# One head per q piece, six rows at a time, and each head's k_m standing twice

## The chip, the cores and the metric

The kernel runs on one core of a Trainium2 chip. Its engines work from queues of their own, each in order: TensorE for matmuls (PE, and PEld for its weight loads), VectorE (DVE), ScalarE (ACT), GpSimd (POOL) and SyncE (SP), which here only issues DMAs. The metric is the device time of one execution in microseconds (us); lower is better. The inputs are the same for both kernels.

## The reference

Three stages follow each other. For each of 8 batches and 8 heads, attention over 576 rows goes through 32 memory slots; its output is the input of a two-layer network (512 to 2048 to 512, squared ReLU), and that one's output goes through a layer of 8 experts in which each of the 4608 tokens takes the best one.

```python
a = exp(phi - max(phi, axis=2)); a = a / (sum(a, axis=2) + 1e-9)     # over the 576 rows
k_m = einsum('bhsm,bhsd->bhmd', a, k)                                 # 32 x 64 per head
v_m = einsum('bhsm,bhsd->bhmd', a, v)
scores = (q @ k_m.T) / 8                                              # 576 x 32 per head
attn = softmax(scores, axis=-1)
x = (attn @ v_m)                                                      # -> [4608, 512]
x = relu(x @ w_in) ** 2 @ w_out
e = argmax(x @ w_gate); g = softmax gate
out = g * (relu(x @ w1[e]) @ w2[e])
```

## The kernel before

A batch's attention is a generator, `attention(b)`, whose steps are spread over the steps of the network's main loop. phi, k and v of a batch come with six neighbouring rows of a head to a partition (96 partitions times 6 rows make the 576). `s_kv(g)` makes k_m and v_m of four heads (a group g); `s_tr(g)` turns them and multiplies by a mask, so that `kb` holds the k_m of two heads at a time as diagonal blocks, and `vbd` the v_m.

q comes in pairs of heads, 4 pairs to a batch and 32 in all (`load_q`, lines 324 to 329). The tile is [96, 6, 2, 64]: for row j of a partition the 64 numbers of one head stand beside the 64 of the other. So the DMA (one for each head, line 328, 144 KB) reads 1536 neighbouring bytes of a partition and writes them as six pieces of 256 bytes. `s_q(pr)` turns a row j of both heads at a time into [128, 96] (line 436) and copies three of these from PSUM (line 441). `s_soft(g)` makes the scores of one half of the rows j for both pairs of a group (line 457: 12 matmuls to a PSUM bank), then the maximum, the subtraction and the exponential of that half (lines 465 to 469), and, after both halves, the sum, the reciprocal and the product (472 to 475). `s_back(g)` turns the result, one half of the rows after the other (line 483), into `attnT`. `u_steps` multiplies v_m into w_in and leaves U (lines 541 to 557), so that a main-loop step n needs U and attnT of the batch whose tokens it reads.

The main loop has 192 steps: 12 blocks of 384 tokens by 16 slices of 128 hidden columns. `g1(n)` is the first layer (line 637, PE; ReLU and squares on ACT at 645 to 648, the low half of g on DVE at 649), and `g2`, three steps behind, adds into three PSUM banks (line 657, 9 matmuls to a step). Ahead of it w_in and w_out come through a ring of four buffers (`raw_ring`, line 215) and are converted from 64-bit numbers (ACT line 234, DVE lines 235 to 237). Beside the main loop runs `weight_stream`: it loads the experts' weights (`wstage`, lines 569 and 571, 512 KB each), finds their maximum or norm (DVE line 180, ACT 588), splits them into two halves of 16 bits (ACT 615, DVE 616) and stores them again (`ws`, line 617). Each block is then routed (`route`): its rows are turned by DMA transposes (line 729), which give the logits (787).

From about 848 us the experts' tiles run (lines 961, 973, 988, 1001, 92), with their DMAs in an order written out by hand.

The order on every other engine is not the order of the code. A scheduler orders all instructions by a model of their durations, DMAs included, and by what they need; then each engine's queue is fixed, SP's too. A DMA that waits for something holds all later ones on SP, and an instruction that waits holds all later ones of its engine. Tiles of one tag in a pool share buffers, and the next user waits for the last reader. Each DMA from SP takes the next of eight completion semaphores in turn.

## Time and profile before

| | |
|---|---|
| median of 3 runs | 1315.33 us (1314.53 to 1315.97) |
| the profiled execution's own time | 1313.53 us |
| its span, first to last instruction | 1311.5 us |
| TensorE clock granted, mean share | 0.953 |
| busy over the span | PE 89%, PEld 47%, DVE 50%, ACT 50%, POOL 9% |
| moved by DMA | 205.25 MB in 264,370 packets, mean 156 GB/s |
| HBM | 234.53 MB read, 55.76 MB written |

Busy shares are means over stages with different limits: loading and converting w_in and w_out (to 103 us), the main loop with attention and the weight stream (to about 600), the main loop almost alone (to 848), the experts. So the views by stretch of time and the chain of waits say more than the shares. A PE span ends where a model says, so a PE that is shown as busy need not be at its peak. A DMA share of 1.0 means that all 16 DMA engines were busy; it can pass 1 somewhat.

### The profile page before, as it was taken

What the parts mean: (1) busy time and instruction counts of PE and PEld (TensorE: products, weight loads), DVE (VectorE), ACT (ScalarE), POOL (GpSimd) and SP (SyncE); (2) the same over time, 40 slices, a digit from 0 to 9 for tenths busy, and PEclk for the clock granted to TensorE, in tenths of its full rate; (3) what the DMA queues carried; (4) which work ended last, traced back from release to release, by engine and by line L of the source; (5) the groups of instructions that cost most, each with busy time, mean ns of one, the idle gap of its engine ahead of it and who ended that gap; (6) DMA issues with size and microseconds to landing.
All of it is one profiled execution on the core that took longest, in us unless ns stands there. A gap on an engine that the chain in (4) does not pass through costs nothing.

```text
span 1311.5 us, 21652 instructions
## 1 busy us (share of the span) xinstructions
PE 1172.5 (89%) x7306; PEld 615.5 (47%) x7306; DVE 659.2 (50%) x1676; ACT 649.6 (50%) x1315; POOL 120.9 (9%) x169
## 2 busy tenths in 40 slices
PE   1537998999998998999999999989999998889896
PEld 0414555545455555466565565434433443334342
DVE  5788977779778767775646344350111111101100
ACT  2458886798777877776656566411111111111111
POOL 2000101101011101011010000031000100000000
PEclk9558998999999998999999999999998999999998
DMA  6956749468879579673131011585467466794762
GB/s 183 261 196 195 198 149 260 153 202 247 222 236 239 195 237 245 188 202 66 25 80 25 25 50 24 164 180 126 105 149 150 97 156 151 159 245 105 157 153 61
DMA packets 264370, 205.25 MB, mean 156 GB/s; under 512 B 209855, under 2 KB 228287, under 8 KB 264256
## 3 DMA queue, kind: packets, MB, share of 16 engines
q1 hardware_dynamic: 257616, 182.67, 55.2%
q0 software_dynamic: 6640, 21.16, 4.6%
q8 instruction: 59, 0.97, 0.3%
q14 instruction: 55, 0.45, 0.1%
HBM read 234.53 MB, written 55.76 MB: 221 GB/s over the span
## 4 chain that ended last, share of the span: by engine, by line
PE 33%; issue 33%; DMA 15%; DVE 9%; ACT 5%; POOL 3%; SPq 0%; POOLq 0%; ACTq 0%; DVEq 0%
PE acc L657 17%; PE h L637 9%; DMA wstage<-in_moe_w_dram 5%; DMA ws<-wo 3%; POOL out_dram L92 3%; DMA raw_ring<-in_moe_w_in_dram 2%; DVE wo L616 2%; DMA e_t<-in_phi_dram 2%; ACT wo L615 1%; DMA xTb<-rec 1%; PE e L961 1%; PE st L457 1%; PE u L541 1%; PE u L550 1%; PE kvm L367 1%
## 5 line engine op out<-in xcount | busy, mean ns | idle before, releaser
L657 PE MATMUL acc<-wo,g 128*128 128x512 f16 x1728 | 419.9, 382 | 1.9 <-ACT x2f L695 1.4
L657 PEld LDWEIGHTS <-g 128*128 128x128 f16 x1728 | 167.4, 99 | 175.1 <-issue 12.4
L988 PE MATMUL e<-w2t,gT 128*128 128x512 f16 x936 | 217.3, 389 | 25.1 <-DMA gT<-g 21.6
L637 PE MATMUL h<-attnT,U 128*128 128x384 f16 (+1 forms) x1536 | 234.6, 290 | 5.6 <-ACT U L556 5.4
L961 PE MATMUL e<-w1t,xT 128*128 128x512 f16 x936 | 210.5, 380 | 8.1 <-DMA w1t<-ws 5.6
L973 DVE SCALAR_TENSOR_TENSOR g<-e,g 128x512 f16<-128x512 f32 x78 | 50.3, 686 | 298.3 <-ACT g L972 298.2
L637 PEld LDWEIGHTS <-U 128*128 128x128 f16 x1536 | 141.5, 100 | 91.5 <-issue 19.4
L988 PEld LDWEIGHTS <-gT 128*128 128x128 f16 x936 | 92.8, 100 | 144.2 <-DMA gT<-g 25.7
L649 DVE TENSOR_TENSOR g<-r,g 128x384 f16<-128x384 f32 x192 | 106.1, 555 | 95.4 <-ACT r L648 94.5
L961 PEld LDWEIGHTS <-xT 128*128 128x128 f16 x936 | 91.4, 98 | 120.7 <-issue 10.0
L645 ACT ACTIVATE r<-h 128x384 f32<-128x384 f32 x192 | 92.6, 485 | 80.4 <-PE h L637 72.6
L1001 ACT ACTIVATE y<-e,fac 128x512 f32<-128x512 f32 x39 | 26.8, 688 | 207.7 <-PE e L988 199.2
L972 ACT ACTIVATE g<-e 128x512 f16<-128x512 f32 x78 | 42.3, 595 | 168.4 <-PE e L961 168.4
L647 ACT ACTIVATE g<-r 128x384 f16<-128x384 f32 x192 | 99.9, 522 | 12.3 <-PE acc L657 8.5
L648 ACT ACTIVATE r<-r 128x384 f32<-128x384 f32 x192 | 99.8, 520 | 3.6
L616 DVE SCALAR_TENSOR_TENSOR wo<-wstage,wsc,wo 128x1024 f16<-128x1024 f32 x64 | 81.0, 1276 | 22.8 <-ACT wo L615 22.8
L615 ACT ACTIVATE wo<-wstage,wsc 128x1024 f16<-128x1024 f32 x64 | 71.9, 1144 | 38.0 <-DMA ws<-wo 21.8
L92 POOL DMA_INDIRECT out_dram<-y,rt x39 | 37.9, 971 | 380.1 <-ACT y L1001 374.2
L92 POOL DMA_INDIRECT scr<-rec,sl x36 | 36.8, 1023 | 281.4 <-ACT r L645 97.9
L367 PE MATMUL kvm<-kv,e_t 128*32 128x128 f32 x768 | 28.2, 293 | 31.8 <-ACT e_t L352 27.4
L180 DVE TENSOR_REDUCE wm<-wstage 128x1 f32<-128x1024 f32 x32 | 38.8, 1212 | 15.4 <-DMA wstage<-in_moe_w_dram 15.4
L457 PE MATMUL st<-kb,qT 128*96 128x64 f32 x384 | 42.0, 266 | 3.5 <-DVE attnT L488 3.5
(241 smaller groups left out, 1077.3 us busy)
## 6 DMA issues: line engine op xcount, KB each, us to landing
w1t<-ws SPq DMA_DIRECT2D x144, 512.0 KB
w2t<-ws SPq DMA_DIRECT2D x144, 512.0 KB
wstage<-in_moe_w_dram SPq DMA_DIRECT2D x64, 512.0 KB
ws<-wo SPq DMA_DIRECT2D x64, 512.0 KB
kv<-in_k_dram SPq DMA_DIRECT2D x16, 576.0 KB
kv<-in_v_dram SPq DMA_DIRECT2D x16, 576.0 KB
q<-in_q_dram SPq DMA_DIRECT2D x64, 144.0 KB
raw_ring<-in_moe_w_in_dram SPq DMA_DIRECT2D x16, 512.0 KB
```

Of the source, the lines that this page charges most:

```text
L92: i = G.indirect_dma_start(out=dst[:, :], out_offset=bass.IndirectOffsetOnAxis(ap=index, axis=0), in_=src, in_offset=None, bounds_check=bo ...
L457: T.matmul(bank[:PS, j * P + 64 * x:j * P + 64 * x + 64], qTs[2 * g + x][:, jj * PS:(jj + 1) * PS], kbd[g][:, 64 * x:64 * x + 64], start=T ...
L615: A.activation(hi, src, AF.Copy, scale=s)
L616: V.scalar_tensor_tensor(lo, src, s, hi, ALU.mult, ALU.subtract)
L637: T.matmul(bank[:, off:off + w], u_t[b][:, g, uh, f * P:(f + 1) * P], attnT[b][:, g, ah, s0:s0 + w], start=(x == 0), stop=(x == len(seq) - 1),
L645: A.activation(r, bank[:, 0:BLK], AF.Relu, scale=2.0 ** -10)
L647: A.activation(g[:, 0], r, AF.Square)
L648: A.activation(r, r, AF.Square)
L649: V.tensor_tensor(g[:, 1], r, g[:, 0], op=ALU.subtract)
L657: T.matmul(a, g[:, gh, tt * P:(tt + 1) * P], wo[:, f, wh, :], start=(f == 0 and x == 0), stop=(f == NF - 1 and x == 2),)
L961: T.matmul(bank[hf], x[:, 4 * xh + c, :].bitcast(F16), w[c][:, wh * F + hf * 512:wh * F + (hf + 1) * 512], start=(c == 0 and xh == 0 and w ...
L988: T.matmul(a, gT[:, 8 * gh + f, :], w[f // 2][:, o:o + DM], start=(f == 0 and x == 0), stop=(f == 7 and x == 2),)
```

## The change

- q of a pair of heads is one tile [96, 2, 6, 64] and one DMA: the six rows of a head stay together, 1536 bytes to a piece.
- `s_q` turns two neighbouring rows of one head at a time, so the upper 64 partitions of a turned piece hold one row and the lower 64 the next.
- `kb` therefore holds each head's k_m twice, over the upper and the lower rows: [128, 4, 2, 32] in place of [128, 128], one multiplication by a broadcast mask.
- `s_soft` goes by pair x of heads in place of halves of the rows: 6 matmuls for a bank from one pair's `qT`, and operations on 4-dimensional strided pieces of `pt`. The numbers of matmuls, ACT and DVE instructions are the same.
- `mx` and `es` share one buffer.

```diff
@@ -323,9 +323,11 @@
 
     def load_q(n):
         b, pr = divmod(n, 4)
-        t = ps.tile([PS, NJ, 2, D], F32, tag="q", name=f"q{n}", bufs=2)
-        for h in range(2):
-            SP.dma_start(t[:, :, h, :], q[b, 2 * pr + h].rearrange("(p j) d -> p j d", p=PS))
+        t = ps.tile([PS, 2, NJ, D], F32, tag="q", name=f"q{n}", bufs=2)
+        SP.dma_start(
+            t.rearrange("p h j d -> p h (j d)"),
+            q[b, 2 * pr:2 * pr + 2].rearrange("h (p j) d -> p h (j d)", p=PS),
+        )
         q_t[n] = t
 
     def over_j(dst, src, op, name):
@@ -338,7 +340,7 @@
     def attention(b):
         last = b == B - 1
 
-        mx = ps.tile([PS, H * M], F32, tag="mx", name=f"mx{b}", bufs=1)
+        mx = ps.tile([P, H * M], F32, tag="mx", name=f"mx{b}", bufs=1)[:PS]
         with tc.issue_after(late[b]) if b in late else ExitStack():
             over_j(mx, e_t[:PS], ALU.max, f"mx{b}")
         mxa = ps.tile([PS, H * M], F32, tag="mxa", name=f"mxa{b}", bufs=1)
@@ -350,7 +352,7 @@
             op=ALU.subtract,
         )
         A.activation(e_t[:PS], e_t[:PS], AF.Exp)
-        es = ps.tile([P, H * M], F32, tag="es", name=f"es{b}", bufs=1)
+        es = ps.tile([P, H * M], F32, tag="mx", name=f"es{b}", bufs=1)
         over_j(es, e_t, ALU.add, f"es{b}")
         yield
         vbd = ps.tile([P, 2, P], F32, tag="vbd", name=f"vbd{b}", bufs=1)
@@ -395,8 +397,14 @@
                 T.transpose(
                     bank[:, i * P:(i + 1) * P], kvn[:, i].rearrange("p a d -> p (a d)"), ident
                 )
-            kb = ps.tile([P, P], F32, tag="kb", name=f"kb{b}_{g}", bufs=2)
-            V.tensor_tensor(kb, bank[:, 0:P], mask, op=ALU.mult)
+
+            kb = ps.tile([P, 4, 2, M], F32, tag="kb", name=f"kb{b}_{g}", bufs=2)
+            V.tensor_tensor(
+                kb,
+                bank[:, 0:P].rearrange("p (h m) -> p h m", h=4).unsqueeze(2).to_broadcast([P, 4, 2, M]),
+                mask[:, 0:2 * M].rearrange("p (x m) -> p x m", x=2).unsqueeze(1).to_broadcast([P, 4, 2, M]),
+                op=ALU.mult,
+            )
             V.tensor_tensor(vbd[:, g, :], bank[:, P:2 * P], mask, op=ALU.mult)
             kbd[g] = kb
 
@@ -430,15 +438,15 @@
             n = 4 * b + pr
             t = q_t.pop(n)
             qT = ps.tile([P, S], F32, tag="qT", name=f"qT{n}", bufs=2)
-            for hf in range(2):
-                bank = side_bank(f"qTp{n}_{hf}")
+            for h in range(2):
+                bank = side_bank(f"qTp{n}_{h}")
                 for j in range(3):
                     T.transpose(
                         bank[:, j * PS:(j + 1) * PS],
-                        t[:, 3 * hf + j].rearrange("p h d -> p (h d)"),
+                        t[:, h, 2 * j:2 * j + 2].rearrange("p a d -> p (a d)"),
                         ident[:PS, :PS],
                     )
-                A.activation(qT[:, hf * 288:(hf + 1) * 288], bank[:, 0:288], AF.Copy)
+                A.activation(qT[:, h * 288:(h + 1) * 288], bank[:, 0:288], AF.Copy)
             if n + 2 < 4 * B:
                 load_q(n + 2)
             qTs[pr] = qT
@@ -449,32 +457,35 @@
             pr = ps.tile([PS, NJ, P], F32, tag="pt", name=f"pt{b}_{g}", bufs=1)
             pt[g] = pr
             st = ps.tile([PS, 2, 3, 12], F32, tag="st", name=f"st{b}_{g}", bufs=2)
-            for hf in range(2):
-                bank = side_bank(f"st{b}_{g}_{hf}")
-                for x in range(2):
+            def half(x):
+                return pr[:, :, 64 * x:64 * x + 64].rearrange("p j (h m) -> p h j m", h=2)
+
+            def each(s):
+                return s.rearrange("p (h j) -> p h j", h=2)
+
+            def spread(s):
+                return each(s).unsqueeze(3).to_broadcast([PS, 2, NJ, M])
+
+            for x in range(2):
+                bank = side_bank(f"st{b}_{g}_{x}")
+                for h in range(2):
                     for j in range(3):
-                        jj = 3 * hf + j
+                        i = 3 * h + j
                         T.matmul(
-                            bank[:PS, j * P + 64 * x:j * P + 64 * x + 64],
-                            qTs[2 * g + x][:, jj * PS:(jj + 1) * PS],
-                            kbd[g][:, 64 * x:64 * x + 64],
+                            bank[:PS, 64 * i:64 * i + 64],
+                            qTs[2 * g + x][:, i * PS:(i + 1) * PS],
+                            kbd[g][:, 2 * x + h].rearrange("p a m -> p (a m)"),
                             start=True, stop=True,
                         )
-                src = bank[:PS, 0:3 * P].rearrange("p (x m) -> p x m", m=M)
-                dst = pr[:, 3 * hf:3 * hf + 3, :].rearrange("p j (h m) -> p (j h) m", m=M)
-                V.tensor_reduce(st[:, hf, 0], src, axis=AX.X, op=ALU.max)
-                V.tensor_tensor(
-                    dst, src, st[:, hf, 0].unsqueeze(2).to_broadcast([PS, 12, M]), op=ALU.subtract
-                )
-                A.activation(dst, dst, AF.Exp, scale=0.125)
-            for hf in range(2):
-                dst = pr[:, 3 * hf:3 * hf + 3, :].rearrange("p j (h m) -> p (j h) m", m=M)
-                V.tensor_reduce(st[:, hf, 1], dst, axis=AX.X, op=ALU.add)
-                V.tensor_scalar(st[:, hf, 1], st[:, hf, 1], EPS, None, ALU.add)
-                V.reciprocal(st[:, hf, 2], st[:, hf, 1])
-                V.tensor_tensor(
-                    dst, dst, st[:, hf, 2].unsqueeze(2).to_broadcast([PS, 12, M]), op=ALU.mult
-                )
+                src = bank[:PS, 0:3 * P].rearrange("p (h j m) -> p h j m", h=2, j=NJ)
+                V.tensor_reduce(each(st[:, x, 0]), src, axis=AX.X, op=ALU.max)
+                V.tensor_tensor(half(x), src, spread(st[:, x, 0]), op=ALU.subtract)
+                A.activation(half(x), half(x), AF.Exp, scale=0.125)
+            for x in range(2):
+                V.tensor_reduce(each(st[:, x, 1]), half(x), axis=AX.X, op=ALU.add)
+                V.tensor_scalar(st[:, x, 1], st[:, x, 1], EPS, None, ALU.add)
+                V.reciprocal(st[:, x, 2], st[:, x, 1])
+                V.tensor_tensor(half(x), half(x), spread(st[:, x, 2]), op=ALU.mult)
 
         def s_back(g):
             for hf in range(2):
```

The scheduler orders the whole program anew. Three places follow; line numbers of the changed kernel differ by up to 17.

SP's queue where the loads of w_out end and the weight stream and batch 1's second group of k and v (the first two `kv` rows) begin, before and then after:

```order
L215 DMA raw_ring_91<-in_moe_w_out_dram 128x1024 x16
L319 DMA kv0_96<-in_k_dram 96x4x384
L319 DMA kv0_96<-in_v_dram 96x4x384
L569 DMA wstage_1578<-in_moe2_w1_dram 128x1024 x2
L328 DMA q6_866<-in_q_dram 96x6x64 x2
L569 DMA wstage_1578<-in_moe2_w1_dram 128x1024 x2
L328 DMA q7_901<-in_q_dram 96x6x64 x2
```

```order
L215 DMA raw_ring_91<-in_moe_w_out_dram 128x1024 x15
L580 DMA wstage_1566<-in_moe2_w1_dram 128x1024 x4
L319 DMA kv0_96<-in_k_dram 96x4x384
L319 DMA kv0_96<-in_v_dram 96x4x384
L327 DMA q6_860<-in_q_dram 96x2x384
L327 DMA q7_894<-in_q_dram 96x2x384
```

The four `wstage` loads now stand ahead of k and v, and each q is one row in place of two.

DVE's queue around the first two pieces of g (`g0`, `g1`, the low halves that `g2` of steps 0 and 1 needs), before and then after; `wm0<-wstage` is the weight stream's first maximum:

```order
L557 SCALAR_TENSOR_TENSOR U0_596<-u0_3_0_627,sb0_593,U0_596 128x512
L649 TENSOR_TENSOR g0_783<-r0_781,g0_783 128x384
L649 TENSOR_TENSOR g1_827<-r1_825,g1_827 128x384
L557 SCALAR_TENSOR_TENSOR U0_596<-u0_3_1_632,sb0_593,U0_596 128x512
L382 TENSOR_SCALAR rs1_0_848<-kvm1_0_805 128x1
L245 TENSOR_REDUCE wo_s_761<-wo_m_92 128x1
```

```order
L568 SCALAR_TENSOR_TENSOR U0_590<-u0_3_0_621,sb0_587,U0_590 128x512
L180 TENSOR_REDUCE wm0_1620<-wstage_1566 128x1
L254 SCALAR_TENSOR_TENSOR wo_87<-wo_87,wo_s_755 128x512
L568 SCALAR_TENSOR_TENSOR U0_590<-u0_3_1_626,sb0_587,U0_590 128x512
L180 TENSOR_REDUCE wm0_1620<-wstage_1566 128x1
L660 TENSOR_TENSOR g0_777<-r0_775,g0_777 128x384
L660 TENSOR_TENSOR g1_821<-r1_819,g1_821 128x384
```

Two instructions that read `wstage` now stand ahead of g0 and g1; before, the first of them stood behind the pieces of g of four steps.

PE's queue behind the last matmul of batch 1's first group (`kvm1_0`), before and then after:

```order
L541 MATMUL u0_3_1_632<-w_in_sb_86,vbd0_208 64x512 x2
L367 MATMUL kvm1_0_805<-kv0_96,e_t_95 32x128 x24
L375 MATMUL kvm1_0_805<-cols_77,es1_798 128x1
L436 MATMUL qTp4_0_856<-ident_75,q4_432 128x96 x3
L436 MATMUL qTp4_1_861<-ident_75,q4_432 128x96 x3
L637 LDWEIGHTS U0_596
```

```order
L369 MATMUL kvm1_0_799<-kv0_96,e_t_95 32x128 x9
L377 MATMUL kvm1_0_799<-cols_77,es1_792 128x1
L668 LDWEIGHTS g0_777
L668 MATMUL acc0_0_947<-wo_87,g0_777 128x512
L668 LDWEIGHTS g0_777
L668 MATMUL acc0_1_948<-wo_87,g0_777 128x512
```

Before, the first layer of steps 4 and 5 (`h4`, `h5`) came next, then three matmuls of g0 and batch 1's second group (`kvm1_1`). Now g0 comes at once, and `kvm1_1` stands after the second layer has gone through more than four steps.

## Rows read from the trace of the kernel before

**Rows 1.** Windows: stretch, length, busy us (instructions) by engine, PE clock, DMA share, GB/s.
```profile
33.00:66.00 33.00, 20.02 (x130) 14.54 (x130) 24.26 (x59) 14.28 (x31) 1.80 (x2) 0.51 1.09 258
66.00:103.00 37.00, 11.59 (x34) 3.18 (x34) 32.59 (x75) 21.11 (x45) 0.80 (x1) 0.50 0.62 208
103.00:600.00 497.00, 472.55 (x3511) 269.97 (x3512) 397.20 (x960) 386.42 (x783) 46.45 (x47) 0.97 0.73 209
600.00:848.00 248.00, 247.53 (x1687) 140.16 (x1686) 116.02 (x352) 147.38 (x319) 16.52 (x17) 1.00 0.20 51
```

**Rows 2.** Windows: two stretches in which q lands, one of k and v.
```profile
13.90:19.80 5.90, 0.00 (x0) 0.00 (x0) 5.82 (x15) 0.12 (x1) 2.82 (x32) 1.00 0.85 173
61.00:65.00 4.00, 2.80 (x18) 2.53 (x18) 3.67 (x9) 1.53 (x4) 1.43 (x1) 0.50 1.15 166
...
123.00:126.00 3.00, 2.37 (x58) 2.20 (x59) 1.54 (x3) 0.95 (x2) 0.00 (x0) 1.00 1.05 358
```

**Rows 3.** DMA issues of the page: from, engine, count, KB each.
```profile
q<-in_q_dram SPq DMA_DIRECT2D x64, 144.0 KB
```

**Rows 4.** The chain of waits in order of time: start, us, what.
```profile
30.19 7.06 DMA raw_ring<-in_moe_w_in_dram
...
52.95 11.61 DMA raw_ring<-in_moe_w_in_dram
...
116.77 6.72 DMA kv<-in_v_dram
...
206.71 9.90 DMA ws<-wo
```

**Rows 5.** Timeline of SP's issues: start, us, what, count (the us run from the first start to the last end).
```profile
31.60 2.28 SPq L328 DMA_DIRECT2D q<-in_q_dram  x2
...
56.12 4.63 SPq L328 DMA_DIRECT2D q<-in_q_dram  x4
...
64.74 41.83 SPq L215 DMA_DIRECT2D raw_ring<-in_moe_w_out_dram  x16
116.39 0.33 SPq L319 DMA_DIRECT2D kv<-in_k_dram  x1
...
117.48 0.82 SPq L569 DMA_DIRECT2D wstage<-in_moe_w_dram  x2
...
210.17 8.74 SPq L328 DMA_DIRECT2D q<-in_q_dram  x4
```

**Rows 6.** Timeline of PE: start, us, what [idle before <- what ended it].
```profile
123.63 1.52 PE L367 MATMUL kvm<-kv,e_t 128*32 128x128 f32 x48 [2.21 <-DMA kv<-in_v_dram]
...
218.54 0.26 PE L787 MATMUL lg<-wg,xTb 128*128 128x16 f16 x4 [4.30 <-ACT qT L441]
```

**Rows 7.** Window of the 7 us behind the second of these.
```profile
218.00:225.00 7.00, 6.46 (x46) 3.86 (x46) 6.77 (x13) 7.00 (x15) 1.96 (x1) 0.52 1.13 308
```

**Rows 8.** Tile wstage: idle time of its engines, ended by what (us, times).
```profile
  DMA wstage<-in_moe_w_dram: 28.8, 22
...
  DMA ws<-wo: 21.8, 17
```

**Rows 9.** Groups by line and shape: busy us, mean ns | idle before.
```profile
L457 PE MATMUL st<-kb,qT 128*96 128x64 f32 x384 | 42.0, 266 | 3.5 <-DVE attnT L488 3.5
...
L475 DVE TENSOR_TENSOR pt<-pt,st 96x384 f32<-96x384 f32 x32 | 17.6, 552 | 0.2
...
L336 DVE TENSOR_TENSOR es<-ojes 128x256 f32<-128x256 f32 x8 | 3.3, 413 | 0.0
```

**Rows 10.** Timeline of 105 to 130 us, PE and DVE.
```profile
114.81 1.52 PE L367 MATMUL kvm<-kv,e_t 128*32 128x128 f32 x48
...
120.61 0.81 PE L657 MATMUL acc<-wo,g 128*128 128x512 f16 x3
...
124.63 1.22 DVE L180 TENSOR_REDUCE wm<-wstage 128x1 f32<-128x1024 f32 x1 [1.38 <-DMA wstage<-in_moe_w_dram]
...
126.08 1.22 DVE L180 TENSOR_REDUCE wm<-wstage 128x1 f32<-128x1024 f32 x1 [0.16 <-DMA wstage<-in_moe_w_dram]
```

## The prediction, made before the changed kernel was run

> **What bounds the kernel now.** I read the windows by stage first [rows 1]. From 33 to 66 us the DMA share is 1.09: loading sets the pace. From 66 to 103 us DVE is busy 32.59 of 37 us, mostly with converting the weights, and DMA only 0.62. From 103 to 600 us PE is busy 472.55 of 497 us, so 24.5 us are idle in plain view, and the mean clock of 0.97 costs about another 0.03 x 497 = 15 us. From 600 to 848 us PE is idle for half a microsecond at full clock and DMA is at 0.20. What comes after reads no q. So a change of the q path can pay ahead of 600 us alone, by the time to PE's first work in the main loop and by some 40 us that PE loses afterwards.
>
> Next, the chain of waits in order of time [rows 4]. Between 30 and 65 us it waits three times for w_in to land; the first took 7.06 and the last 11.61 us. At 116.77 it waits 6.72 us for k and v, and at 206.71 9.90 us for a store of the weight stream. Then SP's issues [rows 5], to see what was on the queue in these waits: two q DMAs at 31.60, four at 56.12, and four from 210.17 on that held SP for 8.74 us. Last, PE's idle gaps [rows 6] and the window behind one of them [rows 7]: 4.30 us idle up to 218.54, and then 7 us at a clock of 0.52.
>
> **The change part by part.**
>
> *The bytes of q.* All 64 q DMAs of 144 KB [rows 3] are 9.4 MB in pieces of 256 bytes; afterwards they are pieces of 1536, as k and v have today. Bandwidth at a full DMA share is the GB/s of a window over its share: where mostly q lands 173/0.85 = 204 and 166/1.15 = 144, where k and v land 358/1.05 = 341 [rows 2]. A pair of heads is 0.295 MB, so it takes 1.45 to 2.05 us of all 16 DMA engines before and 0.86 after. I take a saving of 0.9 us a pair, 28 us for the 32 pairs. The bounds are 0.6, from the better q window, and 1.2, from the worse.
>
> The same windows carry a rule of the Trainium skill, "DMA: Bandwidth & Descriptors", section "Why small descriptors are slow (HBM only)": each packet costs about 3 cycles over its 32-byte beats, 27% for 256 bytes. By it 1536 bytes take 51 cycles in one piece and 66 in six, an estimate of 341 x 51/66 = 264 GB/s for q and a saving of only 0.25 us a pair; the sum below would then be near 4 us in place of 8.5. The windows show q worse than that, so I stay with the windows.
>
> *Ahead of 65 us.* Six pairs are loaded; four of them (the issues from 31.60 to 61 us) fall into the three waits for w_in [rows 4, 5]. 4 x 0.9 = 3.6 us if every microsecond counts. DVE is nearly as loaded behind that, so some of it turns into DVE time: I take 2.5 us. Bounds 0 and 4.8 (4 x 1.2).
>
> *The first blocks.* The new order sends the four wstage loads ahead of k and v. Before, SP stood at the k load until 116.39 us because that waits for PE to be done with the buffer [rows 5], and the loads of the weight stream stood behind it. They can now go right behind the last load of w_out, whose issue ended at 106.57 [rows 5]. And PE no longer meets batch 1's second group before the second layer has gone through four steps, so its wait for k and v [rows 6], 2.21 us, has more than 8 us of work ahead of it. I take 2 us. What is late next is g0: PE now goes to it right behind kvm1_0, and DVE has two readings of wstage ahead of it. That is the rival below; bounds -3.3 (the wait and some smaller gaps beside it) and +9.
>
> *The main loop to 600 us.* A batch brings four pairs, so the burst of k, v, phi and q gets 4 x 0.9 = 3.6 us shorter; batches 6 and 7 load their q where DMA is at 0.20 and nothing waits for it, and batches 2 to 5 are left, 14 us of DMA time. SP also issues half as many q DMAs: the four that took 8.74 us, against 2.28 for two and 4.63 for four elsewhere [rows 5], show SP waiting, and stores of the weight stream stand behind them. The weight stream's engines were idle 28.8 us until a load of wstage landed and 21.8 until a store did [rows 8]; ACT and DVE serve PE in order between these, which is how the store at 206.71 becomes 4.30 us of idle PE at 218.54, and 0.48 x 7 = 3.4 us more at the low clock [rows 6, 7]. Of some 40 us lost by PE I take a tenth, 4 us. Bounds 0 (the gaps move elsewhere in the new order) and 14.
>
> *What is added.* kb grows from 128 to 256 columns; a product of 256 elements took 413 ns [rows 9], so all 16 take 6.6 us of DVE, about half of it there today. DVE has 100 us free of the 497 beside PE [rows 1], so I count none of it. The scores keep their count and shape, 384 matmuls of 64 columns [rows 9]. The softmax steps keep 384 elements, but read and write strided; no row shows that form, so I bound it by the contiguous one's 552 ns below and by twice that above: four operations x 32 x 0.55 = 70 us of DVE at the worst, of which about 60 lie in the main loop. I take nothing: 552 ns for 384 elements against 413 for 256 is 1.09 ns for each further element, a rate at which I see no gain that a contiguous form would have to lose. `s_back` now needs both pairs' products before its first transpose; the second product and its small steps are about 1.5 us later, 16 times. PE has other matmuls in its queue there; I count 0, at most 16 x 1.5 = 24 us.
>
> **The sum.** 2.5 + 2 + 4 = 8.5 us. The profiled execution took 1313.53 us (span 1311.5), 1.8 below the median of the runs; 1313.5 - 8.5 = 1305, and with the 1.8 given back 1307 us.
>
> **The rivals.**
>
> *The weight stream as a whole comes earlier (1299 us).* SP could send wstage from about 106 us, not 117.5: the stream's chain of loads, conversions and stores starts up to 10 us sooner. If that chain and not PE sets the pace until 600 us, the first-block term is 10 and not 2. For it: 50 us of waits for DMA in the stream [rows 8], and the store in the main chain [rows 4]. Against it: its steps stand in the same queues as the main loop's, and PE is 95% busy there [rows 1].
>
> *The saving is hidden (1315 us).* DVE paces the loading from 66 us on [rows 1], and in the main loop the gaps of PE only change places. For it: DVE's 32.59 of 37 us, and that neither of the gaps shown ends with a landing of q. Then the time moves by less than 2.6 us (0.2%, about what a measurement of this kernel can tell from no change).
>
> *DVE stands at wstage ahead of g0 (1320 us).* In the new queue the first layer's g0 comes behind two readings of wstage. In the run before, the first reading began 7.2 us after the first load was issued at 117.48, and the second 1.5 us later [rows 5, 10]. Issued at 106.6 us, the second chunk would be read by 106.6 + 7.2 + 1.5 + 1.2 = 116.5 and g0 ready at 117, a wait of 1 to 4 us for a PE that arrives between 113 and 117 (kvm1_0 ran from 114.81 to 116.33, and startup is to shrink), and no loss against 120.61, when the second layer began before [rows 10]. But if the stream's memory comes free late or the loads share the DMA with the last of w_out, so that the second chunk lands after about 118 us, PE waits up to 9 us, and as h4 and h5 no longer fill the gap, falls to the low clock behind it (3.4 us, [rows 7]). 1307 + 9 + 3.4 = 1319 to 1320. For it: the order is fixed, and PE has nothing else in its queue. Against it: the same order lets w_out's conversion end sooner. Other places of the new order could lose as much; this is the one I can name.
>
> **How the numbers follow.** Forecast (1301 to 1312.7): 0.45. Weight stream earlier (1293 to 1301): 0.17. Hidden (within 2.6 us of 1315.3): 0.16. DVE at wstage, or another loss of the new order: 0.22. So faster 0.62, same 0.16, slower 0.22. The likeliest 1307 us; the range goes from 1295, with about a quarter of the earlier stream's case (0.05) below it, to 1321, which leaves about 0.1 above, for a dearer strided form of DVE and for two losses of the new order at once. Within the forecast's own case the range is 1301 to 1312.7.
>
> **What would show it.** Packets below 512 bytes fall by 36,864 (64 DMAs x 96 partitions x 6), and SP shows 32 issues of q with fewer long ones. The window around 61 us should carry well over 166 GB/s, and the waits for w_in between 30 and 65 us, together, should be 2 to 3 us shorter, with the second layer's first matmul earlier than 120.61 us. PE's wait for k and v at 123.63 should be gone; a new wait of PE's line 657 for g between 112 and 122 us would be the third rival. The DVE softmax groups should stay within 5% of 552 ns; at 600 ns and more the forecast fails by its DVE term. PE's idle time from 103 to 600 us should fall from 24.5 us to about 20, and 848 us should come some 8 us earlier. If the first layer starts no earlier and the second layer's first matmul is still at 120 us, the startup terms were wrong; if both are earlier but the end is not, the main loop's new order gave it back.

## The result, and the profile after

| | before | after |
|---|---|---|
| median, five runs each | 1315.97 us (1314.53 to 1316.86) | 1330.42 us (1324.42 to 1338.04) |
| ratio | | 1.0094 [1.0065, 1.0124] |
| span of the profiled execution | 1311.5 us | 1331.2 us |

Slower by 0.9%, clear of the noise, where 1307 us and faster were forecast. The span is cut here at marks of the timelines: the start, to the second layer's first matmul (`acc`); the loop, from there to the last `acc` of the ninth of twelve blocks, within which most of the attention and nearly all of the weight stream lie; then the last three blocks and the experts. The loop went from 120.6 to 700.5 us before, 579.9 us; after, from 117.8 to 712.0, 594.2 us. The 19.7 us of the two spans are -2.8 in the start, +14.3 in the loop, +0.6 in the last blocks and +7.6 in the experts' stage.

Windows of after, columns and stretches as in [rows 1]:

```profile
33.00:66.00 33.00, 16.27 (x108) 11.00 (x109) 25.98 (x62) 15.03 (x31) 3.44 (x2) 1.00 0.97 281
66.00:103.00 37.00, 13.15 (x55) 6.57 (x53) 35.17 (x80) 21.73 (x45) 0.55 (x1) 0.97 0.66 213
103.00:600.00 497.00, 465.71 (x3434) 266.04 (x3435) 386.21 (x925) 377.15 (x770) 40.20 (x46) 0.98 0.68 204
600.00:848.00 248.00, 245.80 (x1706) 140.82 (x1705) 120.62 (x371) 149.09 (x324) 17.31 (x18) 1.00 0.19 45
```

PE is idle 31.3 us from 103 to 600 us, where it was 24.5 and 20 were forecast; the clock is no lower there. In the loop as cut above PE is idle 32.2 us, 23.8 before; that is 8.4 of the 14.3 us. For the rest it is shown as busy, with some 20 more matmuls that stood ahead of the loop before; this part was not taken apart further. The DMA issues of q, and two windows in which q lands, the second behind the issues at 56.60 and 58.29 us, which answer to [rows 2, 3]:

```profile
q<-in_q_dram SPq DMA_DIRECT2D x32, 288.0 KB
```

```profile
14.00:17.00 3.00, 0.00 (x0) 0.00 (x0) 2.92 (x8) 0.00 (x0) 2.57 (x30) 1.00 1.06 299
60.00:64.00 4.00, 0.00 (x0) 0.00 (x0) 4.00 (x12) 1.91 (x4) 2.33 (x1) 1.00 1.04 335
```

The page counts 172,479 packets under 512 bytes, where it counted 209,855. The windows, with q among other loads as before, carry 299 and 335 GB/s and not 173 and 166. Over their DMA shares that is 282 and 322 GB/s, where [rows 2] gave 204 and 144: 1.05 and 0.92 us a pair, so 0.4 and 1.1 us less than before. So far q's DMA became about what was forecast. The chain of waits (start, us, what), answering to [rows 4]:

```profile
26.18 3.79 DMA raw_ring<-in_moe_w_in_dram
30.43 5.29 DMA raw_ring<-in_moe_w_in_dram
39.19 7.16 DMA raw_ring<-in_moe_w_in_dram
48.22 10.01 DMA e_t<-in_phi_dram
```

The waits for w_in are shorter, 16.2 us together where they were 27.6 (the second of [rows 4]'s three took 8.89), and behind them stands a new one of 10.01 us for phi. SP's issues around 115 us, for [rows 5]:

```profile
111.14 1.75 SPq L580 DMA_DIRECT2D wstage<-in_moe_w_dram  x4
117.63 0.33 SPq L319 DMA_DIRECT2D kv<-in_k_dram  x1
...
119.51 9.46 SPq L327 DMA_DIRECT2D q<-in_q_dram  x2
```

wstage goes ahead of k and v, but two issues of q still hold SP for 9.46 us, as four did for 8.74 at 210 us. The groups by line and shape, for [rows 9]:

```profile
L474 PE MATMUL st<-kb,qT 128*96 128x64 f32 x384 | 43.2, 269 | 3.7 <-DVE attnT L499 3.7
...
L488 DVE TENSOR_TENSOR pt<-pt,st 96x384 f32<-96x384 f32 x32 | 17.2, 541 | 0.1
...
L402 DVE TENSOR_TENSOR kb<-kvT,mask 128x256 f32<-128x256 f32 x16 | 6.6, 414 | 0.2 <-PE kvT L397 0.2
```

Strided or not, 541 ns against 552; none of the other softmax groups takes over 1% longer than before, and of the operations of the scores only kb, twice as wide, became dearer. PE's waits from 103 to 720 us (what for: us, times, longest), of the kernel before and then of the changed one:

```profile
PE h L637 <- ACT U L556: 5.4, 1, 5.4
...
PE st L457 <- DVE attnT L488: 3.5, 1, 3.5
...
PE rk L763 <- DVE oh L750: 1.4, 1, 1.4
...
PE kvT L395 <- DVE kvn L386: 1.0, 2, 0.8
```

```profile
PE kvT L397 <- DVE kvn L388: 7.5, 5, 2.9
PE h L648 <- ACT U L567: 5.7, 1, 5.7
PE qTp L444 <- issue: 5.3, 1, 5.3
PE h L648 <- ACT r L656: 4.1, 3, 2.6
PE rk L774 <- DVE oh L761: 3.5, 2, 3.0
```

The wait for k and v [rows 6] is gone, and none of these is shown to be for a landing of q. The longest that the kernel before does not have, in the timeline of DVE, ACT and PE:

```profile
405.91 0.38 PE L668 MATMUL acc<-wo,g 128*128 128x512 f16 x1
409.48 0.72 ACT L721 ACTIVATE rec<-x2f,sm 128x512 f16<-128x512 f32 x1 [8.73 <-DMA scr<-rec,sl]
409.48 0.15 DVE L789 COPY rec<-tok 128x1 int32<-128x1 int32 x1 [4.95 <-DMA scr<-rec,sl]
409.55 0.54 DVE L481 TENSOR_REDUCE st<-st 96x12 f32<-96x384 f32 x1
...
410.98 0.55 DVE L482 TENSOR_TENSOR pt<-st,st 96x384 f32<-96x384 f32 x1
...
411.63 0.71 PE L444 MATMUL qTp<-ident,q 96*128 96x96 f32 x3 [5.34 <-issue]
```

An instruction of the routing waits on DVE and on ACT for a scatter (`scr`), the softmax stands behind it, and PE is idle for 5.34 us. The profile names no releaser for PE ("issue"); that PE waits for the PSUM bank which the softmax reads is a reading of the times: the gap ends 0.1 us after the subtraction of line 482. Which instruction stands behind which wait is what the order of the queues decides.

### The profile page after: what moved, and what is told of

Its sections match the earlier page's. It is cut to its first block, busy times and chain, and to the rows that moved or that the text cites. A ratio compares the mean times of both kernels' runs of the same rounds, so it can differ in the third digit from the quotient of the medians.

```text
span 1331.2 us, 21616 instructions
## 1 busy us (share of the span) xinstructions
PE 1180.0 (89%) x7306; PEld 619.0 (47%) x7306; DVE 661.4 (50%) x1676; ACT 647.8 (49%) x1315; POOL 118.0 (9%) x169
## 2 busy tenths in 40 slices
DMA packets 233138, 205.24 MB, mean 154 GB/s; under 512 B 172479, under 2 KB 197055, under 8 KB 233024
## 4 chain that ended last, share of the span: by engine, by line
PE 40%; issue 25%; DMA 15%; DVE 11%; ACT 4%; POOL 3%; SPq 1%; POOLq 0%; ACTq 0%; DVEq 0%
PE acc L668 17%; PE h L648 8%; DMA wstage<-in_moe_w_dram 6%; PE e L972 5%; PE e L999 5%; DMA ws<-wo 2%; POOL out_dram L92 2%; DVE wo L627 2%; DMA e_t<-in_phi_dram 2%; DMA xTb<-rec 1%; ACT wo L626 1%; PE u L561 1%; DMA raw_ring<-in_moe_w_in_dram 1%; DMA scr<-rec,sl 1%; DVE wm L180 1%
## 5 line engine op out<-in xcount | busy, mean ns | idle before, releaser
L668 PEld LDWEIGHTS <-g 128*128 128x128 f16 x1728 | 167.4, 99 | 174.9 <-issue 10.6
L999 PE MATMUL e<-w2t,gT 128*128 128x512 f16 x936 | 220.3, 392 | 24.8 <-DMA gT<-g 17.5
L648 PE MATMUL h<-attnT,U 128*128 128x384 f16 (+1 forms) x1536 | 231.3, 288 | 9.9 <-ACT U L567 5.7
L369 PE MATMUL kvm<-kv,e_t 128*32 128x128 f32 x768 | 33.1, 294 | 28.1 <-ACT e_t L354 27.1
L474 PEld LDWEIGHTS st<-kb,qT 128*96 128x96 f32 x384 | 41.8, 186 | 5.6 <-issue 3.2
```

Of the source, the lines that this page charges most:

```text
L474: T.matmul(bank[:PS, 64 * i:64 * i + 64], qTs[2 * g + x][:, i * PS:(i + 1) * PS], kbd[g][:, 2 * x + h].rearrange("p a m -> p (a m)"), star ...
L648: T.matmul(bank[:, off:off + w], u_t[b][:, g, uh, f * P:(f + 1) * P], attnT[b][:, g, ah, s0:s0 + w], start=(x == 0), stop=(x == len(seq) - 1),
L668: T.matmul(a, g[:, gh, tt * P:(tt + 1) * P], wo[:, f, wh, :], start=(f == 0 and x == 0), stop=(f == NF - 1 and x == 2),)
L999: T.matmul(a, gT[:, 8 * gh + f, :], w[f // 2][:, o:o + DM], start=(f == 0 and x == 0), stop=(f == 7 and x == 2),)
```

## The experiments

**Pinning an order.** Twelve kernels were run in an order that is given and not their scheduler's. Every engine's instructions, up to the first of the experts' tiles, are chained in the order of a table, which says for each place in a queue the how-manieth instruction of the code stands there (in short form):

```python
for engine, table in ORDER.items():
    mine = [i for i in traced if i.engine == engine and i.opcode in KEEP[engine]]
    for i, last in consecutive(mine, table):          # no semaphore, only the order of issue
        tc.add_manual_dep(i, last.name, DependencyInfo(NoSync, DATA))
```

Both kernels have the same instructions on PE, DVE, ACT and POOL, one for one, so either can take the other's table; of two places for q on SP one falls out, or one is doubled. An edit of an order is an edit of the table, which the expectation tells. The pin itself is not seen to cost anything: three kernels that are pinned to the old order take 0.9995 to 0.9998 of the kernel before.

All runs, with the loop as above from one trace of each, the ratios from several executions ("rows 0-3" is explained below; "three groups": the softmax of the second half stands just ahead of the transposes in three groups):

| scores | q | order | ratio to before | loop, us |
|---|---|---|---|---|
| before | short | before | 1 | 579.9 |
| changed | long | changed (own) | 1.0093 [1.0058, 1.0129] | 590.5 |
| changed | long, two DMAs | free | 1.0128 [1.0093, 1.0162] | 596.8 |
| changed | long | before, three groups edited | 1.0137 [1.0104, 1.0170] | 597.3 |
| before | short | changed | 1.0163 [1.0129, 1.0196] | 597.3 |
| changed | short | changed | 1.0140 [1.0097, 1.0182] | 599.0 |
| before + wait for both halves | short | before, three groups edited | 1.0141 [1.0093, 1.0188] | 595.0 |
| changed, softmax ahead of weights | long | before, edited | 1.0213 [1.0167, 1.0260] | 608.9 |
| changed, transposes later | long | before, edited | 1.0110 [1.0079, 1.0141] | 588.3 |
| rows 0-3 | long | before, two score matmuls of a group earlier | 0.9998 [0.9979, 1.0017] | 575.5 |
| rows 0-3 | short | the same | 0.9995 [0.9974, 1.0016] | 579.2 |
| rows 0-3 | long | free | 1.0092 [1.0063, 1.0120] | 597.8 |
| rows 0-3 | short | free | 1.0105 [1.0067, 1.0143] | 592.6 |
| before, mixed rows | long | before | 0.9909 (other experts) | 580.9 |
| before, mixed rows | long | free | 0.9938 (other experts) | 582.0 |
| before, wider product | short | free | 1.0006 [0.9980, 1.0031] | 583.0 |
| before, wider product | short | before | 0.9997 [0.9970, 1.0024] | 582.7 |
| rows 0-3, phi later | long | before, edited | 1.0005 [0.9981, 1.0028] | 577.5 |
| rows 0-3, phi and a weight copy later | long | before, edited | 1.0010 [0.9986, 1.0035] | 577.1 |

**The two kernels and the two orders.**

The first three take one kernel's code and one kernel's table; the fourth is the changed kernel with

```diff
-        SP.dma_start(t.rearrange("p h j d -> p h (j d)"), ...)
+        for h in range(2):
+            SP.dma_start(t[:, h].rearrange("p j d -> p (j d)"), q[b, 2 * pr + h].rearrange("(p j) d -> p (j d)", p=PS))
```

> The changed kernel once more, for a second profile. Theory 1 (the loss comes from the order in which the scheduler put the instructions of the main loop): 1324 to 1334 us, with the same places late again, and block 7's last accumulation near 645 us where the kernel before has it at 635.7. Theory 2 (an operation of the change costs more): the same time, so this run does not tell the two apart. Theory 3 (a good part of the loss lies in the experts' stage and varies from one execution to the next): this profile's experts' stage, from block 11's end on, takes 464 to 468 us as in the kernel before and not 472, and the main loop is still some 10 us late.

> The changed kernel's operations, all of them, with every engine's queue pinned to the order of the kernel before (a table in the kernel gives the order; in three groups the softmax of the second half is put just ahead of the transposes that now need it). Theory 1 (order): the loss is gone, and the cheaper q pieces remain: 1306 to 1316 us, DVE's softmax groups still 546 ns. Theory 2 (the operations): 1324 to 1332 us, as the changed kernel. Theory 3 (the experts' stage varies): main loop 10 us earlier than the changed kernel's at 700 us, total anywhere from 1308 to 1322.

> The kernel before, all of its operations, with every engine's queue pinned to the order of the changed kernel; where that has one DMA for q, two stand one behind the other. Theory 1 (order): slower than before by as much as the changed kernel or more, since the costly q pieces are back and the first half of the scores now waits in PE's queue for both pairs: 1326 to 1345 us. Theory 2 (the operations): 1310 to 1318 us. Theory 3: main loop within 4 us of the kernel before's at 700 us.

> The changed kernel with q in two DMAs of 144 KB, one for each head, in the same long pieces; the scheduler is free and orders 434 of 6666 matmuls and 256 of 1676 DVE instructions differently from the changed kernel. Theory 1 (order): a time of its own, off the changed kernel's by more than 2 us in either direction (1312 to 1336), though the work differs by 32 issues on a queue that is 5% busy. Theory 2 (the operations): the changed kernel's time within 2 us, since every operation of its scores is there. Theory 3: within 4 us of it, with the difference in the experts' stage.

Measured: 1329.8, 1334.3, 1336.8 and 1333.2 us, the kernel before 1316.9 beside them. The old operations in the new order lose 20 us, with the waits that the changed kernel has; here of that run, PE, 103 to 720 us:

```profile
PE kvT L395 <- DVE kvn L386: 7.8, 4, 3.2
PE h L637 <- ACT U L556: 6.9, 2, 6.5
PE qTp L436 <- issue: 5.2, 1, 5.2
```

So the new order costs by itself. (In it the old scores have a need that it was not laid out for, both pairs for the first bank; the changed scores in the same order with the same short pieces, below, still take 1.0140.) But theory 1 said that the old order would give the loss back, and it did not: the new operations lose 17 us in it, and one wait stands out. In the run `changed_old_order`, PE's wait (us, times, longest), and then its timeline and DVE's:

```profile
PE aT L494 <- DVE pt L488: 19.2, 4, 8.0
```

```profile
238.66 1.15 PE L474 MATMUL st<-kb,qT 128*96 128x64 f32 x12
...
249.12 0.74 PE L494 MATMUL aT<-ident,pt 96*128 96x96 f32 x3 [8.01 <-DVE pt L488]
```

```profile
238.63 0.56 DVE L488 TENSOR_TENSOR pt<-pt,st 96x384 f32<-96x384 f32 x1
240.74 1.22 DVE L180 TENSOR_REDUCE wm<-wstage 128x1 f32<-128x1024 f32 x1 [1.56 <-DMA wstage<-in_moe_w_dram]
241.88 1.27 DVE L627 SCALAR_TENSOR_TENSOR wo<-wstage,wsc,wo 128x1024 f16<-128x1024 f32 x1
243.07 0.55 DVE L660 TENSOR_TENSOR g<-r,g 128x384 f16<-128x384 f32 x1
243.54 0.55 DVE L481 TENSOR_REDUCE st<-st 96x12 f32<-96x384 f32 x1
244.01 1.27 DVE L627 SCALAR_TENSOR_TENSOR wo<-wstage,wsc,wo 128x1024 f16<-128x1024 f32 x1
245.20 1.21 DVE L180 TENSOR_REDUCE wm<-wstage 128x1 f32<-128x1024 f32 x1
...
248.51 0.55 DVE L488 TENSOR_TENSOR pt<-pt,st 96x384 f32<-96x384 f32 x1
```

The first product (line 488) is done at 239.2 us. In the kernel before, this was all that the first transposes `aT` needed. Now they need the second, which ends at 249.06, behind four steps of the weight stream (5.0 us) and a wait of 1.56 us for one of its loads. This is the longest of the four waits. In the others, 4.4, 3.8 and 3.0 us at 345, 453 and 642 us, no step of the weight stream stands between the two products, only other steps of the attention, g, and waits for ACT; at the second, DVE had waited 2.78 us for phi ahead of both products. Theory 2 in its form "an operation is dearer" is out too: the groups keep their durations (above; and the kernel without the dependency, below, loses nothing in the old order). Two DMAs for q are no better than one; that run is 3.3 us above the changed kernel at intervals that overlap, and so does not tell the theories apart.

**The dependency, the pieces, and a repair.** The first of these is the kernel before with the changed `load_q` and the transposes of the first cut, the second is the kernel before with one dependency added (second cut) in the order of `changed_old_order`, the fourth is the changed kernel with q laid down in short pieces (third cut):

```diff
-                        t[:, 3 * hf + j].rearrange("p h d -> p (h d)"),
+                        t.rearrange("p h j d -> p (h j d)")[:, (3 * hf + j) * P:(3 * hf + j + 1) * P],
```

```diff
+ tc.add_manual_dep(turn.ins, product[g].ins.name, DependencyInfo(Sync, DATA))   # each transpose of s_back
```

```diff
+        for h in range(2):
+            SP.dma_start(t[:, h, ::-1], q[b, 2 * pr + h].rearrange("(p j) d -> p j d", p=PS))
```

> The kernel before in its own order, with the changed kernel's q DMA alone (one for a pair, pieces of 1536 bytes). The transposes then take the same count of columns from where the rows now stand, so the scores mix the rows of one head, and the output is not the reference's; every operation has its shape and place. Theory 1 (order, and what stands ahead of what): the cheaper q is a small gain or nothing: 1308 to 1317 us, the median of the kernel before being 1316.9. Theory 2 (an operation of the change costs): if the long DMA is the one that costs, 1325 us or more; if it is the scores, 1308 to 1317.

> The kernel before with the order of the run before it that pinned the changed kernel to the old order, and one thing added: the transposes of the attention matrix wait for the products of both halves, as the changed kernel's must. Theory 1 in its narrower form (the order was made for transposes that need one half only; the second half's softmax stands behind steps of the weight stream that wait for DMAs): 1326 to 1336 us, PE's waits for the product some 19 us where the kernel before has none. Theory 2 in the form that the strided softmax, the larger kb or the q DMA costs: 1314 to 1320 us.

> The changed kernel in the order of the kernel before, with the steps of the weight stream that stood between a group's first and last softmax step on DVE or ACT moved behind the last one, in seven groups, wherever no deadlock follows. Theory 1 (narrower form): PE's waits for the product fall from 19 us to under 8, and the time from 1334 to 1316 to 1324 us, though the weight stream is held up. Theory 2: within 3 us of 1334. A rival: the weight stream, held up, makes its own waits, and the time stays at 1328 to 1336 with other waits in place of these.

> The changed kernel in its own order with q in pieces of 256 bytes again, two DMAs for a pair (the six rows of a head are laid down last first, and the transposes of the attention matrix take them so; the result is the reference's). Beside the kernel before in the new order (1336.8) and the changed kernel (1329.8) it splits the 7 us between them. If the q pieces make them: 1335 to 1339 us, waits for w_in longer by 2 to 3 us. If the scores' new dependency makes them (the first bank needs one pair only): 1328 to 1332.

Measured: 1303.4, 1334.8, 1345.0 and 1332.8 us, before 1315.0. The wait, with no other part of the change and in the same order, makes the whole loss of `changed_old_order`, 1.0141 against 1.0137; the kernel before has no such wait in this stretch:

```profile
PE aT L483 <- DVE pt L475: 19.3, 4, 8.7
```

The repair failed, and further than the rival had it: the time rose above its range, and the wait for the product did not shrink. At the first of the four places no step of the weight stream stands between the products on DVE any more, but the softmax waits for its exponential on ACT, which stands behind a copy of the weight stream that waits for a store. PE's wait in that run, and then lines of ACT and DVE:

```profile
PE aT L494 <- DVE pt L488: 21.6, 4, 7.3
```

```profile
254.72 1.15 ACT L626 ACTIVATE wo<-wstage,wsc 128x1024 f16<-128x1024 f32 x1 [2.48 <-DMA ws<-wo]
...
256.69 0.55 DVE L485 TENSOR_REDUCE st<-pt 96x12 f32<-96x384 f32 x1 [2.81 <-ACT pt L483]
```

The 1303.4 us look like the gain that was forecast and are not: the loop took 580.9 us, as before, and the experts' stage 454.1, for 464.4 in the kernel before. In that stage only the data differ: mixed scores send tokens to other experts. That run told nothing of the total. The last one lies between its two partners. Against the changed kernel, which has the long pieces in the same order, it is 0.0047 slower, good to 0.0055, or 6 us good to 7: in this order a gain of 8.5 us, as forecast, is not excluded, nor is none.

**A kernel without the dependency.** Half a bank more gives the scores back their order by rows: the first bank takes rows 0 to 3 of all four heads (512 columns), the second rows 4 and 5, with the same 12 matmuls and the same number of DVE and ACT steps.

```diff
-            for x in range(2):
-                bank = side_bank(f"st{b}_{g}_{x}")
+            for r0, r1 in ((0, 4), (4, 6)):
+                bank = side_bank(f"st{b}_{g}_{r0}")
+                out4 = bank[:PS, :].rearrange("p (j a n) -> p j a n", a=2, n=P)
...
-                            bank[:PS, 64 * i:64 * i + 64],
+                            out4[:, j - r0 // 2, :, 32 * (2 * x + h):32 * (2 * x + h) + 32],
```

> All of the change (long q pieces, one DMA, k_m twice, the shared buffer), but the scores of a group go by rows again: one bank holds rows 0 to 3 of both pairs (512 columns), the other rows 4 and 5, so that the transposes of rows 0 to 2 need the first bank's softmax alone, as in the kernel before. The queues are pinned to the order of the kernel before, only two score matmuls of a group stand earlier. Theory: the loss of 17 to 20 us in this order comes from the transposes that wait for both banks. Then PE's wait for the product is gone and the time is the kernel before's less what q saves: 1305 to 1316 us. If the loss has another cause in the change (k_m twice, the long DMA, one head for each piece), it stays at 1328 to 1336.

> The same with q in pieces of 256 bytes and two DMAs for a pair (rows laid down last first), in the same order: the pair of runs prices the q pieces alone on right data, which the run with mixed heads could not do, since its tokens went to other experts. If the pieces pay as predicted, 5 to 9 us more than the run with long pieces; if they are hidden in this order, within 3 us of it.

> The changed kernel with its own scores, pinned to the order of the kernel before, with the transposes of the first half of the rows (and their copies on ACT and DVE) moved to just ahead of those of the second half, where both halves were ready in the kernel before. Theory (the transposes stand too early for a product that now comes later): PE's wait for the product goes from 19 us to under 6 and the time from 1334 to 1308 to 1320. Rival: the second half is late itself, since its place was chosen while the first half filled the time; then 1320 to 1332.

> The first-four-rows kernel in the order that the scheduler gives it by itself. If the dependency is what costs, whatever the order, it comes near the pinned one: 1305 to 1320 us. If any order that is not the kernel before's costs some 15 us (as the kernel before's own operations lost 20 in the changed kernel's order), 1322 to 1336.

Measured: 1315.4, 1315.2, 1331.5 and 1328.6 us, before 1316.1. With the dependency out, the rest of the change costs nothing in the old order, and PE's longest waits are the old ones (shown above; [rows 6] has the one for qT):

```profile
PE h L651 <- ACT U L570: 5.3, 1, 5.3
PE lg L801 <- ACT qT L449: 3.0, 1, 3.0
PE st L471 <- DVE attnT L502: 2.8, 1, 2.8
```

Long pieces against short ones in the same order: 0.9998 and 0.9995. Each is good to about 0.002, the difference to 0.0028 or 3.7 us, so in this order the 8.5 us of the forecast are excluded. By the rule of the Trainium skill that the prediction weighed ("DMA: Bandwidth & Descriptors", section "Why small descriptors are slow (HBM only)") the sum would, by an estimate from the page's figure, have been near 4 us; nothing is seen of these either. Moving the first transposes back came out in the rival's range, 1331: the wait for the product is gone, and others stand in its place, the longest here; whether the second half is late itself, as the rival had it, was not taken apart.

```profile
PE st L474 <- DVE attnT L499: 7.8, 2, 5.7
```

And in its free order the repaired kernel is as slow as the changed one, with other waits, PE, 103 to 720 us:

```profile
PE kvT L397 <- DVE kvn L388: 8.6, 5, 5.4
...
PE h L651 <- ACT r L659: 4.3, 5, 1.5
```

The long-piece runs of this kernel in the two orders price an order alone: the same instructions differ by 0.0094, or 12 us.

**What leads the scheduler there.** The wider product is this edit, with `mx` and `es` sharing a buffer:

```diff
-            kb = ps.tile([P, P], F32, tag="kb", name=f"kb{b}_{g}", bufs=2)
-            V.tensor_tensor(kb, bank[:, 0:P], mask, op=ALU.mult)
+            kb = ps.tile([P, 2, P], F32, tag="kb", name=f"kb{b}_{g}", bufs=2)
+            V.tensor_tensor(kb, bank[:, 0:P].unsqueeze(1).to_broadcast([P, 2, P]),
+                            mask.unsqueeze(1).to_broadcast([P, 2, P]), op=ALU.mult)
+            kb = kb[:, 0]
```

> The kernel before with one product for each group twice as wide (k_m times the mask, 256 columns, the second half never read) and the shared buffer that makes room for it; the scheduler is free. DVE has 16 x 0.15 = 2.4 us more in all. If any edit lays the program out anew at a loss: 1323 to 1334 us (793 of 6666 matmuls stand elsewhere than before). If it takes the q load or the scores of the change to lead the scheduler astray: 1314 to 1320.

> The same kernel pinned to the order of the kernel before. Both theories: 1314 to 1319 us, the wider product being hidden on DVE. If it is over 1322, the wider product itself costs, and the run in the free order says nothing of the order.

> The first-four-rows scores with q in pieces of 256 bytes, two DMAs for a pair, in the scheduler's free order; in the old order it took 1315.2 us, and with long pieces in the free order 1328.6. If the long q load is what leads the scheduler astray: 1313 to 1319 us. If the transposes by one head and the scores do: 1325 to 1333.

> The kernel before with the long q load alone (one DMA for a pair; the transposes take mixed rows, so its tokens go to other experts and only its partner in the old order, 1303.4 us or 0.9909 of the kernel before, is a measure), in the scheduler's free order. If the long q load leads the scheduler astray: 1314 to 1320 us, 1.000 to 1.004. If the scores do: 1301 to 1307.

Measured: 1317.0, 1314.3, 1326.6 and 1305.5 us, the kernel before 1315.3 beside the first two and 1313.6 beside the others. So not every new order loses: 793 moved matmuls cost nothing. In the free order the long load alone costs 0.9938 - 0.9909 = 0.0029, good to 0.0044 and so not clear of nothing. What is left as costing is one-head transposes and scores by row pairs in the free order, by the ratios 14 us with short pieces and 12 with long ones (good to 6 and 5). Which of their lengths or needs the scheduler's model answers to was not taken apart. PE's waits of the third run are yet others, behind the routing's `rec`:

```profile
PE kvT L395 <- DVE rec L790: 6.9, 2, 5.9
```

**An attempt to win with it.** In the old order DVE waits for phi three times ahead of a softmax.

> The kernel with rows 0 to 3 in the first bank, in the old order (1315.4 us), and in batches 2, 3 and 5 the maximum over phi moved 8, 5 and 6 places later in DVE's queue. It waited there 2.9, 2.3 and 3.9 us for phi to land, with a softmax and the low half of g behind it. If PE's stalls at 216, 334 and 510 us (3.0, 2.7 and 2.8 us) come from it, they fall to under 1 us each and the time to 1306 to 1312. If the next wait in the queue takes their place: 1313 to 1318.

> The same, and on ACT one copy of the weight stream moved three places later, behind two copies of qT; it waited 4.1 us at 213 us for a store. If ACT and not DVE held PE at 216 us, the stall there goes only in this run: 2 to 3 us less than the run without it. If DVE held it, the same time within 1.5 us.

Measured: 1315.8 and 1316.7 us against 1315.3, no gain. The 3.0 us at 216 us stayed in the first run; in the second they went, and others came, here as PE's waits of the two:

```profile
PE lg L801 <- ACT qT L449: 3.0, 1, 3.0
```

```profile
PE h L651 <- ACT r L659: 5.8, 5, 2.2
```

No version with the reference's result ran faster than the kernel before.

## Why the prediction was wrong, step by step

- **The main loop** (-4, bounds 0 to 14) is the step that failed in the kernel as it ran. Its worst case was 0, "the gaps move elsewhere in the new order": the sum gave the new order no way to lose in the loop. The loop took 14.3 us longer, and 10.6 in the second profile. The prediction had "another loss of the new order" among its rivals, but named one place, g0 behind wstage, where nothing was lost: the second layer began at 117.8 us, not late. The losses were spread: `kvT`, `rk`, `qTp`, ReLU. The new order alone cost the old operations 1.0163, and the kernel with rows 0 to 3 in the first bank takes 0.9998 in the old order and 1.0092 in its scheduler's. Nor did the cheaper q show in the loop: with long and short pieces in the old order it took 575.5 and 579.2 us in one profile each, and the timed pair shows nothing. That q's 14 us of DMA time lay where no engine waited for them is the likely reason, and not shown by itself.
- **What is added** (0) failed in the old order. The prediction saw that "`s_back` now needs both pairs' products before its first transpose", put the bound at 24 us, and counted 0, because "PE has other matmuls in its queue there". The queue is in order: the other matmuls stand behind the waiting one, and PE is idle (8.01 us up to 249.12 us). By itself, in the old order with three groups edited, this cost 1.0141, or 18.5 us. The price of 1.5 us each, 16 times, had the wrong shape as well: four waits of 3.0 to 8.7 us made 19.3, the longest where the weight stream stood on DVE between the two products.
- **What joins the two is open.** The changed kernel does not show that wait in its loop, since the scheduler laid the program out anew. Without the dependency the free order still lost 12 us, so no share of the measured loss is shown to be the dependency's; which of the new needs of the transposes and scores leads the scheduler to a dear order was not found.
- **Ahead of 65 us** (-2.5): the waits for w_in did get shorter, by 11.3 us, and phi's 10.0 took their place. The first layer began at 103.4 us and, in the second profile, at 106.4, where it had begun at 102.9; the second layer at 117.8 and 120.8. By the prediction's own sign the startup terms were wrong. The start ended between 116.8 and 126.4 us over all profiles, without relation to the pieces: 122.5 and 119.5 for long and short in one order.
- **The first blocks** (-2): the wait for k and v went, but the second layer's earlier start was partly only a changed order: 313 matmuls stand ahead of it, not 336. It was no sign of a gain, though the prediction took it for one.
- **The bytes of q.** The 341 GB/s that the prediction took from 123 to 126 us are not those of k and v: of the 1064 packets of that window 852 are under 512 bytes and the others 2 KB or more, so no piece of 1536 bytes lands in it. The term came out about right all the same (0.4 and 1.1 us a pair in two windows, for 0.9), which is partly luck; in the old order none of it is seen in the time.
- **Right:** the count of packets (37,376 fewer for 36,864), well over 166 GB/s where q lands behind 56 us (335), kb at 414 ns and the softmax within 5%. The closing sentence named the loop's new order as what would give a gain back; its condition, an earlier first layer, was not met.
- **Not settled:** the changed kernel's experts' stage took 472.0 and 470.7 us in its two profiles, 464.4 before and 464.5 with the changed operations in the old order; the other profiles with the reference's result lie between 463.8 and 469.4. Nothing of the change runs there.

## What to carry to other kernels

Before counting a new dependency at nothing, look at what stands between the old and the new releaser in the releaser's queue, waits included; its price can be all of that, and not the length of the operation. Where a scheduler orders the program, an edit has two prices, its own and that of the new order, and only a run pinned to the old order tells them apart. An experiment with wrong data is read by the stage that does not depend on the data.

## What was not expected of the hardware

In the old order the pieces of q could be made six times as long (a window with them carries 335 GB/s where one before carried 166) with no effect on the time within 3.7 us, although the DMA share stood at 1.09 in the stretch that the chain of waits crosses [rows 1, 4]. And single executions of one program spread more than a forecast of 8 us likes: the kernel before from 1307.1 to 1326.8 us (from 1307.7 in one session), the changed one from 1324.0 to 1338.0, so differences under some 4 us needed a dozen executions on each side.
